# Two of eight norms transposed half on TensorE and half by DMA, a third normalized on GpSimd, in a fused adaLN transformer block

## The chip, the core and the metric

The kernel runs on one core of one Trainium2 chip. Its time is the device time of one execution in microseconds; a lower time is better. The core's engines work side by side, each through its own list of instructions in order, and wait for each other by semaphores: TensorE (PE, matrix products, with weight loads listed as PEld), VectorE (DVE), ScalarE (ACT), GpSimd (POOL) and SyncE (SP), which here only issues DMAs.

## What is computed

The reference is a transformer block over 2048 positions of 512 features: a modulated layer norm, an attention over 8 earlier positions spaced by 2, a gated residual, a second modulated layer norm, a gated GELU feed-forward network with 1792 inner features, and a second gated residual.

```python
mod = (_silu(c) @ w_mod).reshape(c.shape[0], 6, 1, -1)
sa, ca, ga, sb, cb, gb = (mod[:, 0].copy(), ..., mod[:, 5].copy())
h = _layernorm(x, axis=-1) * (1 + ca) + sa
x = x + ga * _A_ref(h, A_wqkv, A_wo)
h = _layernorm(x, axis=-1) * (1 + cb) + sb
x = x + gb * _B_ref(h, B_w_gate, B_w_up, B_w_down)
...
# in _A_ref: 32 heads of 16, window W = 8, dilation 2
idx = pos[:, None] - off[None, :]
mask = idx >= 0
logits = jnp.einsum('bhsd,bhswd->bhsw', q, kg) * scale
logits = jnp.where(mask[None, None, :, :], logits, -1000000000.0)
attn = _softmax(logits, axis=-1)
o = jnp.einsum('bhsw,bhswd->bhsd', attn, vg)
```

## The kernel before

The 2048 positions are worked in four blocks (`sg` 0 to 3) of 512; a block has four chunks of 128 positions, one per `c4`. Each block goes through these steps, and the steps of different blocks overlap:

- **Layer norm 1** (`LN1.sg`): mean and variance of each chunk, by DVE (L430, L431) or by ACT with two accumulating passes (L408, L419); the table `ACT_CH` says which chunks ACT takes. POOL raises the variance to the power of -1/2 (L471, "the root"). DVE subtracts and scales each chunk into `xn` (L448). Then `xn` is transposed so that features lie on partitions, and each of the four groups of 128 features is scaled and shifted by the modulation into `hT`.
- **Transposes.** There are three ways. Block 0's first norm is transposed on PE in two halves (`transp0`, L509) and evicted from PSUM with the scaling by ACT (L545) and DVE (L543). A norm named in `BY_PE` (LN1.1 and LN2.0) is transposed by sixteen PE instructions (L484), and ACT evicts and scales it in four instructions (L527). Every other norm is transposed by one DMA that SP issues (L490); then ACT (L527) or, for LN1.2, POOL (L525) scales `hT` in place.
- **qkv** (L580, L598): groups of four matmuls each, evicted by ACT into `qT`, `kT` and `vT`. `vT` goes to DRAM and comes back in four shifted copies as `V` (L630, L639).
- **Logits**: DVE multiplies q by the shifted k (L659, "the products", `pq`), four times per block; PE sums over the head's features into PSUM (L673). For block 0, DVE adds a mask of large negative numbers to the first 16 positions (L685). Maximum, difference, exponential, sum and division follow on DVE and ACT (L690 to L717).
- **Values**: DVE multiplies the weights by V (L766, "the value products"), PE sums (L780), ACT copies (L791), PE applies `wo` (L801), DVE adds x (L810).
- **Layer norm 2** (`LN2.sg`), in the same way as norm 1, into `h2T`.
- **Feed-forward**: PE's gate and up groups (L834), ACT's GELU and copy (L868, L875), DVE's product (L886), PE's down projection (L846, L858), DVE's residual (L893), SP's store.

At the start PE runs matmuls on a constant tile, the warm-ups (L217), between the first real ones; 32 small matmuls (L348) make the modulation of norm 1.

The order is written out. Every step is a small operation in a generator, and the list `ORDER` names, one number per operation, whose generator goes next. All engines' instructions are emitted in that one order, so each engine's own list is the part of `ORDER` that belongs to it. `take` and `give` count the buffers of a pool; `after` names what must be done. SP's list matters as a queue: it issues loads, stores and DMA transposes one behind the other, and one that waits holds up all behind it. The weights' loads are `Wg` and `Wu` (1792 KB each) and `Wd`.

Of the kernel before, what the change touches and what calls it, by code (L numbers as in the profile page):

```python
# [9 lines left out]
ALU = mybir.AluOpType  # L10
# [96 lines left out]
def kernel(  # L107
# [49 lines left out]
    maskT = const.tile([H, W, 16], F32, name="maskT")  # L157
# [63 lines left out]
    def loads():  # L221
# [28 lines left out]
        def mb(n):  # L250
            return n / 0.333
# [74 lines left out]
    def mods():  # L326
# [15 lines left out]
        for b in (1, 0):  # L342
# [8 lines left out]
            yield Op("PE", 0.43, f, after=[f"wm{b}", "scT", "w15"], take=[SL["mm"]] if b else [],  # L351
# [86 lines left out]

    def norm_x(key, src, ev, parts=((0, 4),)):
        aa, ab = ACT_CH.get(ev, (0, 0))  # L440
        dv = [c4 for c4 in range(CPS) if not aa <= c4 < ab]
        for c4 in range(CPS):
            def f(c4=c4):
                k = norm_tiles(ev)
                if c4 == 0:
                    B[key] = T("xn", [P, CPS, D], BF16, "xn")
                m, o = (k["mv"][:, c4, 0:1], ALU.subtract) if c4 in dv else (k["s"][:, 1, c4:c4 + 1], ALU.add)
                nc.vector.tensor_scalar(out=B[key][:, c4, :], in0=src()[:, c4, :], scalar1=m,  # L448
                                        scalar2=k["rstd"][:, c4:c4 + 1], op0=o, op1=ALU.mult)
            yield Op("DVE", 0.325, f, after=[f"{ev}.rs{max(a for a, b in parts if a <= c4)}"],  # L450
# [24 lines left out]
    def transp(key, dkey, dtag, ev):  # L475
        if ev in BY_PE:
            for dtp in range(2):
                def f(dtp=dtp):
                    hp = T("att", [P, CPS, 2, P], BF16, "hTp")
                    B[key, dtp] = hp  # L480
                    for c4 in range(CPS):
                        for dd in range(2):
# [3 lines left out]
                         fire=f"{ev}.t{dtp}")  # L486
        else:
# [8 lines left out]
    BY_PE = ('LN1.1', 'LN2.0')  # L496
# [17 lines left out]
    def transp_ev(key, dkey, dtag, sc, bi, ev, dep):  # L514
        pe = ev in BY_PE
        for dtp in range(2):
            for dd in range(2):
                dt = 2 * dtp + dd

                def f(dt=dt, dtp=dtp, dd=dd):  # L520
# [5 lines left out]
                    else:  # L526
# [4 lines left out]
                         give=[SL["att"]] if pe and dd == 1 else [], fire=f"{ev}.h{dt}")  # L531

# [19 lines left out]
    def ln1(sg):  # L552
        ev = f"LN1.{sg}"
        yield from norm(lambda: B["x", sg], lambda c4: [f"x0.{c4 // 2 * 2}"] if sg == 0 else [f"x{sg}"], ev,
                        PARTS0 if sg == 0 else ((0, 4),))
# [3 lines left out]
    def ln1_x(sg):  # L559
        yield from norm_x(("xn1", sg), lambda: B["x", sg], f"LN1.{sg}", PARTS0 if sg == 0 else ((0, 4),))  # L560
# [407 lines left out]
```

## Time and profile before

| what | us |
|---|---|
| median of three runs | 237.67 |
| the three runs | 237.32, 237.67, 238.6 |
| the profiled execution | 237.21 |
| its span, first to last instruction | 235.0 |
| TensorE's granted clock | 1.0 of full speed |

The profile's page gives each engine's busy time and the chain of work that ended last. On a timeline row come the start, the time of the group from its first start to its last end, the engine, the line, the operation, the tiles (written<-read), the shapes and the count; in brackets the engine's idle time before it and what ended it. All times in rows are microseconds from the span's start. A row of the chain has start, time, engine, tile and line.

### The profile page before, as it was taken

To read this page: it belongs to the slowest core of one execution; us is meant where nothing else is said; L and a number is where in the kernel's file an instruction comes from. 1 tells how busy PE (TensorE), PEld (TensorE's weight loads), DVE (VectorE), ACT (ScalarE), POOL (GpSimd) and SP (SyncE) were. 2 spreads that over 40 slices of the span, in tenths; PEclk is the share of its full clock that TensorE was granted. 3 is DMA by queue.
4 is the path that set the end of the run, shared out by engine and by line. 5 is a ranking of instruction groups with operands and counts; after the bars stand their busy time and mean duration, and the time that the engine had idled before them with its cause. 6 is when DMAs were issued, how large, how long until landed. Compare 5 with 4: busy or idle time off the path is not lost.

```text
span 235.0 us, 3679 instructions
## 1 busy us (share of the span) xinstructions
PE 230.8 (98%) x1387; PEld 108.4 (46%) x1387; DVE 170.1 (72%) x238; ACT 150.9 (64%) x286; POOL 17.9 (8%) x43
## 2 busy tenths in 40 slices
PE   7999999999999999999999999999999999999995
PEld 2656454444644444444444444444444444444443
DVE  3899999999969999999899899279296211322222
ACT  4899997887996659937647862447636733367400
POOL 2612351000100000100000010000001000000000
PEclk9999999999999999999999999999999999999999
DMA  6998999999975859753100895320002210000011
GB/s 213 374 267 277 214 207 177 246 307 360 199 184 157 295 149 208 121 113 100 59 0 4 157 196 99 120 62 0 0 3 40 50 45 22 25 0 0 0 47 45
DMA packets 36265, 30.21 MB, mean 129 GB/s; under 512 B 14872, under 2 KB 34328, under 8 KB 36248
## 3 DMA queue, kind: packets, MB, share of 16 engines
q1 hardware_dynamic: 35968, 29.72, 50.7%
q8 instruction: 11, 0.18, 0.3%
q10 hardware_dynamic: 280, 0.26, 0.3%
q14 instruction: 6, 0.05, 0.1%
HBM read 22.37 MB, written 4.98 MB: 116 GB/s over the span
## 4 chain that ended last, share of the span: by engine, by line
PE 96%; ACT 2%; DVE 0%; issue 0%
PE u_ps L834 21%; PE g_ps L834 21%; PE y_ps L846 19%; PE qkv_ps L598 16%; PE x_ps L801 6%; PE LTp L673 3%; PE o_ps L780 3%; PE warm_ps L217 3%; PE y_ps L858 1%; PE hTp L484 1%; PE qkv_ps L580 1%; ACT hT L545 1%; ACT gl L419 1%; ACT LTp L701 0%; PE modT_ps L305 0%; PE modT_ps L348 0%
## 5 line engine op out<-in xcount | busy, mean ns | idle before, releaser
L834 PE MATMUL g_ps<-h,Wg 128*128 128x512 bf16 x224 | 57.5, 379 | 0.0
L834 PE MATMUL u_ps<-h,Wu 128*128 128x512 bf16 x224 | 57.5, 379 | 0.0
L868 ACT ACTIVATE gl<-g_ps 128x512 bf16<-128x512 f32 x56 | 33.5, 599 | 25.4 <-PE g_ps L834 22.1
L875 ACT CAST ub<-u_ps 128x512 bf16<-128x512 f32 x56 | 32.8, 586 | 21.4 <-PE u_ps L834 21.3
L846 PE MATMUL y_ps<-Wd,hht 128*128 128x512 bf16 x210 | 46.3, 379 | 0.0
L598 PE MATMUL qkv_ps<-hT,wqkv 128*128 128x512 bf16 x184 | 41.8, 380 | 0.1
L886 DVE TENSOR_TENSOR hht<-gl,ub 128x512 bf16<-128x512 bf16 x56 | 22.6, 420 | 25.2 <-ACT ub L875 23.2
L659 DVE TENSOR_TENSOR pq<-qT,kT 128x4096 bf16<-128x4096 bf16 x16 | 36.2, 2284 | 0.3 <-PE o_ps L780 0.2
L766 DVE TENSOR_TENSOR pv<-PT,V 128x4096 bf16<-128x4096 bf16 x16 | 35.9, 2283 | 0.0
L834 PEld LDWEIGHTS <-Wu 128*128 128x128 bf16 x224 | 21.6, 98 | 27.2 <-issue 1.9
L834 PEld LDWEIGHTS <-Wg 128*128 128x128 bf16 x224 | 21.6, 98 | 27.1 <-issue 1.7
L846 PEld LDWEIGHTS <-hht 128*128 128x128 bf16 x210 | 20.6, 98 | 24.8
L598 PEld LDWEIGHTS <-wqkv 128*128 128x128 bf16 x184 | 20.3, 114 | 19.6 <-issue 2.3
L893 DVE TENSOR_TENSOR ot<-y_ps,x 128x512 bf16<-128x512 f32 x15 | 10.3, 688 | 22.9 <-PE y_ps L846 22.9
L471 POOL TENSOR_TENSOR rstd<-rstd,neghalf 128x4 f32<-128x4 f32 (+1 forms) x9 | 8.9, 990 | 151.0 <-DVE rstd L460 81.3
L801 PE MATMUL x_ps<-woP,oT 128*128 128x512 bf16 x64 | 15.1, 379 | 0.0
L430 DVE BATCH_NORM_STATS2 st<-x 128x6 f32<-128x512 bf16 x18 | 12.3, 685 | 3.2 <-DMA x<-in_A_x_dram 2.9
L810 DVE TENSOR_TENSOR x<-x_ps,x 128x512 bf16<-128x512 f32 x16 | 10.8, 678 | 3.6 <-PE x_ps L801 3.4
L527 ACT ACTIVATE h<-h,modT,scl 128x512 bf16<-128x512 bf16 x12 | 8.8, 803 | 6.8 <-DMA h<-xn 6.8
L791 ACT CAST oT<-o_ps 128x512 bf16<-128x512 f32 x16 | 9.1, 590 | 3.5 <-PE o_ps L780 3.5
L620 ACT CAST kT<-qkv_ps 128x512 bf16<-128x512 f32 x16 | 9.6, 599 | 1.5 <-PE qkv_ps L598 1.4
L801 PEld LDWEIGHTS <-oT 128*128 128x128 bf16 x64 | 6.9, 109 | 7.1 <-issue 0.4
(84 smaller groups left out, 184.8 us busy)
## 6 DMA issues: line engine op xcount, KB each, us to landing
V<-vscr SPq DMA_DIRECT2D x12, 520.0 KB, 9.4
wm<-in_w_mod_dram SPq DMA_DIRECT2D x6, 512.0 KB, 5.9
vscr<-vT SPq DMA_DIRECT2D x4, 512.0 KB, 4.5
out_dram<-ot SPq DMA_DIRECT2D x15, 128.0 KB, 1.7
Wg<-in_B_w_gate_dram SPq DMA_DIRECT2D x1, 1792.0 KB
Wu<-in_B_w_up_dram SPq DMA_DIRECT2D x1, 1792.0 KB, 18.4
wqkv<-in_A_wqkv_dram SPq DMA_DIRECT2D x3, 512.0 KB, 8.5
x<-in_A_x_dram SPq DMA_DIRECT2D x3, 512.0 KB, 7.6
```

The source lines that it names most:

```text
L430: nc.vector.bn_stats(out=st[:], in_=src()[:, c4, :])
L598: nc.tensor.matmul(ps[:], lhsT=wqkv[blk][:, dt, j::4], rhs=B["hT", sg][:, :, dt, :], start=(dt == 0), stop=(dt == DT - 1))
L659: nc.vector.tensor_tensor(out=pq[:], in0=_ap(B["qT", sg][:, j, :], [[0, W], [1, SG]]), in1=_ap(kT[:, j, sg * SG + 2:sg * SG + 2 + SG], [[2 ...
L766: nc.vector.tensor_tensor(out=t[:], in0=_ap(B["PT", sg][:, 0, :], [[SG, 2], [0, 4], [1, SG]]), in1=_ap(v[:, 0, j, :], [[8, 2], [4 * (SG + ...
L801: nc.tensor.matmul(ps[:], lhsT=B["oT", sg][:, j, c4::CPS] if sg else B["oT", sg][:, j, c4 * P:(c4 + 1) * P], rhs=woP[:, j, :], start=(j == ...
L810: nc.vector.tensor_tensor(out=x[:, c4, :], in0=B["x1ps", sg, c4][:], in1=x[:, c4, :], op=ALU.add)
L834: nc.tensor.matmul(ps[:], lhsT=Wt[:, dt, ft * P:(ft + 1) * P], rhs=B["h2T", sg][:, :, dt, :], start=(dt == 0), stop=(dt == DT - 1))
L846: nc.tensor.matmul(ps[:], lhsT=B["hh", sg, ft][:, c4 * P:(c4 + 1) * P], rhs=B["Wd", ft // 4][:, ft % 4, :], start=(ft == 0), stop=(ft == F ...
L868: nc.scalar.activation(out=gl[:], in_=B["g", sg, ft][:], func=ACT.Gelu_apprx_tanh)
L875: nc.scalar.copy(out=ub[:], in_=B["u", sg, ft][:])
L886: nc.vector.tensor_tensor(out=hh[:], in0=B["gl", sg, ft][:], in1=B["ub", sg, ft][:], op=ALU.mult)
L893: nc.vector.tensor_tensor(out=ot[:], in0=B["y", sg, c4][:], in1=B["x", sg][:, c4, :], op=ALU.add)
```

## The change

- **Half and half.** LN1.1 and LN2.0 leave `BY_PE` and enter `HALF`. Chunks 0 and 1 of `xn` are transposed by a DMA on SP, into half of `hT` (or `h2T`), and scaled there in place by four POOL instructions of 128x256 (`half_ev`). Chunks 2 and 3 are transposed by eight PE instructions into one PSUM tile, and ACT evicts and scales them in four instructions of 128x256. Their norm runs in two parts, each with its own root on POOL. The first matmuls of the block wait for both halves; ACT's evictions wait for both transposes.
- **LN1.3's normalization** (four instructions) moves from DVE to POOL (`X_POOL`).
- **The mask** is a bf16 tile on 128 partitions and is added in PSUM by two small matmuls with an identity, inside the sum of block 0's first logits; the DVE addition goes.
- **The head.** The second half of block 0's x is loaded by SP's queue, second in it, and no longer by ACT's. The warm-ups are 17 in place of 20: ten, three and three ahead of the last modulation matmuls and one behind block 0's transposes, where it was eleven, five and one ahead, two between the halves of the transposes and one behind.
- **The order** of everything is a new list. On POOL, the root of LN1.2 stands between the first and the second scaling of LN1.1. On SP, LN1.1's transpose stands between two weight loads ahead of x of block 3; LN2.0's stands behind the first V load of block 1 and `Wu`, where `Wu` came before that block's V loads. The modulation matmuls of norm 2, the two gate computations and the value sums move a little; the number of the other instructions is the same.

```diff
-    maskT = const.tile([H, W, 16], F32, name="maskT")
+    maskT = const.tile([P, W, 16], BF16, name="maskT")
...
-            yield Op("ACT", 0.46, ldx(0, 2, 4, nc.scalar), fire="x0.2", lat=mb(0.25), dma=True)
...
             yield Op("SP", 0.47, ldx(0, 0, 2), fire="x0.0", lat=mb(0.25))
+            yield Op("SP", 0.47, ldx(0, 2, 4), fire="x0.2", lat=mb(0.25))
...
+    X_POOL = ("LN1.3",)
...
-                nc.vector.tensor_scalar(out=B[key][:, c4, :], in0=src()[:, c4, :], scalar1=m,
-                                        scalar2=k["rstd"][:, c4:c4 + 1], op0=o, op1=ALU.mult)
+                (nc.gpsimd if ev in X_POOL else nc.vector).tensor_scalar(
+                    out=B[key][:, c4, :], in0=src()[:, c4, :], scalar1=m, scalar2=k["rstd"][:, c4:c4 + 1], op0=o, op1=ALU.mult)
...
+        elif ev in HALF:
+            def f():
+                B[dkey] = T(dtag, [P, CPS, DT, P], BF16, dtag)
+                nc.sync.dma_start_transpose(out=B[dkey][:, 0:2].rearrange("p c d s -> p (c d) s"),
+                                            in_=B[key][:, 0:2].rearrange("p c d -> p (c d)"))
+            yield Op("SP", 1.65, f, after=[f"{ev}.x1"], take=[SL[dtag]], fire=f"{ev}.t", lat=0.5)
+
+            def f():
+                B[key, 0] = T("att", [P, DT, 2, P], BF16, "hTp")
+                for dt in range(DT):
+                    for c4 in range(2):
+                        nc.tensor.transpose(B[key, 0][:, dt, c4, :], B[key][:, 2 + c4, dt * P:(dt + 1) * P], ident[:])
+            yield Op("PE", 0.445, f, after=[f"{ev}.x3", "ident"], take=[SL["att"]], give=[SL["xn"]], fire=f"{ev}.t1")
...
-    BY_PE = ('LN1.1', 'LN2.0')
+    BY_PE = ()
+
+    HALF = ('LN1.1', 'LN2.0')
+
+    HALF_POOL = ('LN1.1', 'LN2.0')
...
+        if ev in HALF:
+            for dt in range(DT):
+                def f(dt=dt):
+                    nc.scalar.activation(out=B[dkey][:, 2:4, dt, :], in_=B[key, 0][:, dt, :, :], func=ACT.Identity,
+                                         scale=sc(dt), bias=bi(dt))
+                yield Op("ACT", 0.455, f, after=[f"{ev}.t1", f"{ev}.t"] + dep, give=[SL["att"]] if dt == DT - 1 else [],
+                         fire=f"{ev}.h{dt}")
+            return
...
+    def half_ev(dkey, sc, bi, ev, dep):
+        for dt in range(DT):
+            def f(dt=dt):
+                o = B[dkey][:, 0:2, dt, :]
+                if ev in HALF_POOL:
+                    nc.gpsimd.tensor_scalar(out=o, in0=o, scalar1=sc(dt), scalar2=bi(dt), op0=ALU.mult, op1=ALU.add)
+                else:
+                    nc.scalar.activation(out=o, in_=o, func=ACT.Identity, scale=sc(dt), bias=bi(dt))
+            yield Op("POOL" if ev in HALF_POOL else "ACT", 0.44 if ev in HALF_POOL else 0.47, f, after=[f"{ev}.t"] + dep,
+                     fire=f"{ev}.hp{dt}")
...
+                        if sg == 0 and j == 0:
+                            nc.tensor.matmul(B["LT", 0][0:H, 4 * t:4 * t + 4, 0:16], lhsT=ident[:, 0:H],
+                                             rhs=maskT[:, 4 * t:4 * t + 4, :], start=False, stop=False, tile_position=(0, 0))
...
-        if sg == 0:
-            def f():
-                L = B["LT", 0][0:H, :, 0:16]
-                nc.vector.tensor_tensor(out=L, in0=L, in1=maskT[:], op=ALU.add)
-            yield Op("DVE", 0.32, f, after=["lp.0", "consts"], fire="lm.0")
...
-    pl.spawn(warmup(13, 20))
+    pl.spawn(warmup(13, 17))
```

More of the change, by code (lines that the diff above doesn't have):

```diff
@@ L350, in f @@
                                          start=(kt == 0), stop=(kt == 3))
-            yield Op("PE", 0.43, f, after=[f"wm{b}", "scT", "w15"], take=[SL["mm"]] if b else [],
+            yield Op("PE", 0.43, f, after=[f"wm{b}", "scT", "w11"], take=[SL["mm"]] if b else [],
                      give=[] if b else [SL["prod"]], fire=f"mp{b}")
@@ L447, in f @@
                 m, o = (k["mv"][:, c4, 0:1], ALU.subtract) if c4 in dv else (k["s"][:, 1, c4:c4 + 1], ALU.add)
-                nc.vector.tensor_scalar(out=B[key][:, c4, :], in0=src()[:, c4, :], scalar1=m,
-                                        scalar2=k["rstd"][:, c4:c4 + 1], op0=o, op1=ALU.mult)
-            yield Op("DVE", 0.325, f, after=[f"{ev}.rs{max(a for a, b in parts if a <= c4)}"],
+                (nc.gpsimd if ev in X_POOL else nc.vector).tensor_scalar(
+                    out=B[key][:, c4, :], in0=src()[:, c4, :], scalar1=m, scalar2=k["rstd"][:, c4:c4 + 1], op0=o, op1=ALU.mult)
+            yield Op(*(("POOL", 0.77) if ev in X_POOL else ("DVE", 0.325)), f, after=[f"{ev}.rs{max(a for a, b in parts if a <= c4)}"],
                      take=[SL["xn"]] if c4 == 0 else [], fire=f"{ev}.x{c4}")
@@ L554, in ln1 @@
         yield from norm(lambda: B["x", sg], lambda c4: [f"x0.{c4 // 2 * 2}"] if sg == 0 else [f"x{sg}"], ev,
-                        PARTS0 if sg == 0 else ((0, 4),))
+                        PARTS0 if sg == 0 or f"LN1.{sg}" in HALF else ((0, 4),))
     PARTS0 = ((0, 2), (2, 4))
     def ln1_x(sg):
-        yield from norm_x(("xn1", sg), lambda: B["x", sg], f"LN1.{sg}", PARTS0 if sg == 0 else ((0, 4),))
+        yield from norm_x(("xn1", sg), lambda: B["x", sg], f"LN1.{sg}", PARTS0 if sg == 0 or f"LN1.{sg}" in HALF else ((0, 4),))
     def ln1_ev(sg):
@@ L564, in ln1_ev, with ln1_evh @@
                              f"LN1.{sg}", ["mod01"])
+    def ln1_evh(sg):
+        yield from half_ev(("hT", sg), lambda d: mod01[:, 4 + d:5 + d], lambda d: mod01[:, d:d + 1], f"LN1.{sg}", ["mod01"])
     def ln1_ev0(onv):
@@ L601, in qkv @@
             tk = {0: [SL["q"]], 1: [], 2: [SL["vs"]]}[blk] if j == 0 else []
-            yield Op("PE", 0.865, f, after=[f"LN1.{sg}.h{d}" for d in (("0.1", "1.0", "3.1") if sg == 0 else (2, 3))] + [f"wqkv{blk}"], take=[SL["mm"]] + tk,
+            yield Op("PE", 0.865, f, after=[f"LN1.{sg}.h{d}" for d in (("0.1", "1.0", "3.1") if sg == 0 else (2, 3))] + ([f"LN1.{sg}.hp3"] if f"LN1.{sg}" in HALF else []) + [f"wqkv{blk}"], take=[SL["mm"]] + tk,
                      give=[SL["hT"]] if last else [], fire=f"qp.{sg}.{blk}.{j}")
@@ L814, in ln2 @@
         ev = f"LN2.{sg}"
-        yield from norm(lambda: B["x", sg], lambda c4: [f"x1.{sg}.{c4}"], ev)
+        yield from norm(lambda: B["x", sg], lambda c4: [f"x1.{sg}.{c4}"], ev, PARTS0 if ev in HALF else ((0, 4),))
     def ln2_x(sg):
-        yield from norm_x(("xn2", sg), lambda: B["x", sg], f"LN2.{sg}")
+        yield from norm_x(("xn2", sg), lambda: B["x", sg], f"LN2.{sg}", PARTS0 if f"LN2.{sg}" in HALF else ((0, 4),))
     def ln2_ev(sg):
@@ L822, in ln2_ev, with ln2_evh @@
                              lambda d: modT[:, d:d + 1], f"LN2.{sg}", ["mod3", "mod4"])
+    def ln2_evh(sg):
+        yield from half_ev(("h2T", sg), lambda d: scl[:, d:d + 1], lambda d: modT[:, d:d + 1], f"LN2.{sg}", ["mod3", "mod4"])
     LAST = ((0, 384), (384, 512))
     def ffn_mm(sg):
-        h2 = [f"LN2.{sg}.h3"]
+        h2 = [f"LN2.{sg}.h3"] + ([f"LN2.{sg}.hp3"] if f"LN2.{sg}" in HALF else [])
         for ft in range(FT):
@@ L930 @@
         for n, g in (("sa1", lambda q: norm_act(lambda: B["x", q], lambda c4: [f"x{q}"] if q else ["x0.2", "x0.0"], f"LN1.{q}")),
-                     ("sa2", lambda q: norm_act(lambda: B["x", q], lambda c4: [f"x1.{q}.{c4}"], f"LN2.{q}")), ("ln1", ln1), ("ln1x", ln1_x), ("t1", lambda q: transp(("xn1", q), ("hT", q), "hT", f"LN1.{q}") if q else transp0(("xn1", 0), "LN1.0")), ("h1", lambda q: ln1_ev(q) if q else ln1_ev0(False)), ("qkv", qkv),
+                     ("sa2", lambda q: norm_act(lambda: B["x", q], lambda c4: [f"x1.{q}.{c4}"], f"LN2.{q}")), ("ln1", ln1), ("ln1x", ln1_x), ("t1", lambda q: transp(("xn1", q), ("hT", q), "hT", f"LN1.{q}") if q else transp0(("xn1", 0), "LN1.0")), ("h1", lambda q: ln1_ev(q) if q else ln1_ev0(False)), ("h1h", lambda q: ln1_evh(q) if f"LN1.{q}" in HALF else iter(())), ("h2h", lambda q: ln2_evh(q) if f"LN2.{q}" in HALF else iter(())), ("ln2a", lambda q: rst(f"LN2.{q}", 0, 2, []) if f"LN2.{q}" in HALF else iter(())), ("qkv", qkv),
                      ("qev", qkv_ev), ("v", vload), ("pq", logits), ("lmm", logits_mm), ("soft", soft), ("ptd", lambda q: pt_dma(q) if q in PT_DMA else iter(())), ("pv", pv), ("pvmm", pv_mm), ("pvev", pv_ev), ("x1mm", x1_mm),
```

71 rows, old and new, of the table ORDER are left out of this document.

## The prediction

> **What bounds the kernel now.** I read the page's header and chain of waits first, then the list of what TensorE (PE) waited for.
>
> ```profile
> span 235.0 us, 3679 instructions
> PE 230.8 (98%) x1387; PEld 108.4 (46%) x1387; DVE 170.1 (72%) x238; ACT 150.9 (64%) x286; POOL 17.9 (8%) x43
> ```
>
> ```profile
> engine line waited for: us in total, times, longest us
> PE warm_ps L217 <- DVE gB L212: 1.2, 1, 1.2
> PE qkv_ps L580 <- ACT hT L545: 0.2, 1, 0.2
> ```
>
> PE is busy for 98% and after the first 11 us waits for nobody. So every microsecond of PE work removed is gained, and every new wait in front of PE is paid in full. The profiled execution took 237.21 us: the span and 2.2 us around it. The median of the runs, 237.67, is 0.46 above it. The windows of ten microseconds say where a second engine is full too:
>
> ```profile
> 20.00:30.00 10.00, 10.00 (x111) 5.48 (x110) 10.00 (x9) 9.94 (x26) 2.52 (x1) 1.00 0.89 215
> 40.00:50.00 10.00, 10.00 (x90) 4.94 (x90) 10.00 (x5) 7.94 (x14) 0.00 (x0) 1.00 0.96 214
> ```
>
> After the window's length come PE, weight loads, DVE, ACT and POOL, then the clock, the DMA share and GB/s. From 20 to 30 us DVE is as full as PE: whatever delays DVE there reaches PE.
>
> **Head: 17 warm-ups, x on one queue.**
>
> ```profile
> 1.24 4.88 PE L217 MATMUL warm_ps<-gB 128*128 128x512 bf16 x11 [1.24 <-DVE gB L212]
> 9.23 1.48 ACT L545 ACTIVATE hT<-hTp,mod 128x256 bf16<-128x256 bf16 x3 [0.92 <-PE hTp L509]
> 9.44 0.73 DVE L543 TENSOR_SCALAR hT<-hTp,mod 128x256 bf16<-128x256 bf16 x2 [0.30 <-PE hTp L509]
> 10.31 1.05 DVE L543 TENSOR_SCALAR hT<-hTp,mod 128x256 bf16<-128x256 bf16 x3 [0.15 <-PE hTp L509]
> 10.76 1.80 PE L580 MATMUL qkv_ps<-hT,wqkv 128*128 128x256 bf16 x15 [0.16 <-ACT hT L545]
> 12.39 0.81 PE L598 MATMUL qkv_ps<-hT,wqkv 128*128 128x512 bf16 x3
> ```
>
> A cold warm-up costs 4.88/11 = 0.44. The new order has 16 instead of 17 ahead of the last modulation matmuls, so the ACT evictions can start at 9.23 - 0.44 = 8.8 and end at 10.3. Four pairs of 256-wide matmuls remain behind the third of them; at (12.39 - 10.76)/15 = 0.109 each that is 0.87, and L598 could start at 11.2 instead of 12.39. DVE no longer has two warm-ups between its two groups: 9.0 + 0.73 + 1.05 = 10.8, against 11.36. I take -0.9 for PE, with -0.4 (the one cold warm-up, if the modulation weights land later behind one more load in SP's queue) and -1.2 as ends; DVE is 0.55 ahead.
>
> **Transposes taken from PE.** LN1.1 and LN2.0 keep half of their sixteen transposes on PE:
>
> ```profile
> 20.50 0.89 PE hTp L484 x16
> 62.48 0.47 PE hTp L484 x8
> 63.81 0.45 PE hTp L484 x8
> 28.34 0.98 PE LTp L673 x16
> ```
>
> Half of 0.89 is -0.45, and half of 0.47 + 0.45 is -0.46. The mask costs PE two matmuls of 64 columns; a 512-column one of the same tile costs 0.98/16 = 0.06, so both are between 0 and 0.12, taken as +0.1. What DVE loses with it (0.28) comes below. Widening the mask's memsets falls into POOL's idle time before its first reciprocal root. These PE terms sum to -0.9 - 0.91 + 0.1 = -1.7.
>
> **LN1.1's other half: SP, then POOL, then DVE.** The new chain is: two normalized chunks, a DMA transpose of half size, four POOL scalings of 256 elements (`hp0` to `hp3`), then the first qkv group of block 1. On POOL the root of LN1.2 stands between `hp0` and `hp1`, and DVE's four normalizations of LN1.2 wait for that root; behind them stand the products `pq`, which PE's logits need.
>
> ```profile
> 18.20 1.05 DVE L448 TENSOR_SCALAR xn<-x,mv,rstd 128x512 bf16<-128x512 bf16 x3
> 18.37 1.25 POOL L471 TENSOR_TENSOR rstd<-rstd,neghalf 128x4 f32<-128x4 f32 x1 [3.15 <-DVE rstd L465]
> 20.95 8.89 DVE L659 TENSOR_TENSOR pq<-qT,kT 128x4096 bf16<-128x4096 bf16 x4
> 27.48 3.00 POOL L525 TENSOR_SCALAR hT<-hT,mod 128x512 bf16<-128x512 bf16 x1 [7.87 <-PE qkv_ps L598]
> L525 POOL TENSOR_SCALAR hT<-hT,mod x4: 768/769/3002, 27.5 to 32.0; 128x512 bf16<-128x512 bf16 x4
> hT<-xn SPq DMA_TRANSPOSE x2, 4.4
> ```
>
> Before, this root (1.25) ran beside LN1.1's normalizations. Now the LN1.1 ones come earlier in DVE's queue and nothing independent is left: DVE stands idle for one root, +1.2. Second, the scalings. The first L525 scaling, started at 27.48 under the last of four products, took 3.00 instead of 0.77 and ended about one scaling after the product's end at 29.84: one engine kept the other out. Half-size scalings cost half of 0.77, say 0.4. `hp1` to `hp3` are ready at the very moment at which DVE's normalizations are; one of the two must wait, so DVE's products start between 0 and 2.2 (what that one scaling lost) later. I take the three scalings end to end, +1.2.
>
> The Trainium skill (SBUF — State Buffer, "Who interferes with whom") says that a DVE instruction with two SBUF inputs, or a `tensor_scalar` in a two-port mode, and a GpSimd instruction reading SBUF shut each other out for a whole instruction, whoever is first. The 3.00 us row agrees for the products; no row isolates the normalizations. By the page this term is the full 1.2; if normalizations don't collide it is 0.
>
> The third product of the four ended at 20.95 + 3 x 8.89/4 = 27.6. Now it ends at 27.6 - 0.55 + 1.2 + 1.2 = 29.5. PE needed it at 28.34 + 0.49 = 28.8 and now arrives at 28.8 - 0.9 - 0.45 + 0.1 = 27.6. **Stall: 1.9** (0.7 without exclusion). This contains any wait of PE at the first qkv group, a little earlier. All that holds if the half transpose lands in time for `hp0`: a full one takes 4.4, a half one between 2.2 and 4.4, taken as 3.2; at 4.4 it delays the root, and DVE, by another 0.8.
>
> **The third norm on POOL and the mask, in between.**
>
> ```profile
> 29.76 0.28 DVE L685 TENSOR_TENSOR LTp<-LTp,maskT 32x128 f32<-32x128 f32 x1
> 37.14 1.28 DVE L448 TENSOR_SCALAR xn<-x,sums,rstd 128x512 bf16<-128x512 bf16 x4
> 38.50 2.87 SPq L490 DMA_TRANSPOSE hT<-xn  x1
> 48.15 2.71 PE qkv_ps L598 x12
> ```
>
> DVE is relieved of 0.28 + 1.28 = 1.56, which eats most of its 1.85 delay before the value products. LN1.3's normalizations take 4 x 0.77 = 3.1 on POOL, so its transpose is issued about 1 us later than 38.50, or 3 if a product gets in between. Block 3's matmuls start in the L598 group at 48.15, after one group of block 2, at 49.0; transpose (4.4) and ACT's four scalings (2.8 below) after 39.5 end at 46.7. The cover is 2.3 us. I cost it at nothing; were it gone, at most 1.
>
> **LN2.0's other half.**
>
> ```profile
> 44.85 0.97 SPq L223 DMA_DIRECT2D Wu<-in_B_w_up_dram  x1
> Wu<-in_B_w_up_dram SPq DMA_DIRECT2D x1, 1792.0 KB, 18.4
> 50.63 4.01 SPq L639 DMA_DIRECT2D V<-vscr  x3
> V<-vscr SPq DMA_DIRECT2D x1, 520.0 KB, 6.3
> 58.00:60.00 2.00, 2.00 (x12) 1.02 (x9) 1.90 (x6) 2.00 (x5) 0.18 (x1) 1.00 1.10 206
> 60.87 0.73 DVE L448 TENSOR_SCALAR xn<-x,sums,rstd 128x512 bf16<-128x512 bf16 x2
> 63.04 2.79 ACT L527 ACTIVATE h<-hTp,modT,scl 128x512 bf16<-128x512 bf16 x4
> 65.99 0.86 PE g_ps L834 x4
> ```
>
> SP's queue changes here: Wu's load now stands behind the first V load of block 1, which waits for the block's V buffer (issued at 50.63), and directly ahead of the half transpose. Wu landed at 44.85 + 18.4 = 63.25 with the DMA engines full. With one V load ahead (520 KB at 206 GB/s: 2.5) it lands near 65.8, and the transpose, if it goes through the same queue behind it, near 66.5. If it overtakes, it is issued right after the first two normalizations, which end at 61.6 today and up to one root (1.2) earlier if their root is taken ahead of the other pair's, and lands 3.2 later, at 63.6 to 64.8. Behind the landing come POOL's four scalings (1.6) and, in parallel, ACT's four half evictions, which wait for the same landing (2.79 for full ones; about 1.9 for half). So the first g matmul can start between 65.5 and 68.5; PE arrives at 65.99 - 1.25 + 1.9 - 0.46 = 66.2. Stall between 0 and 2.3; I take **1.8**, as Wu's row, the nearest, shows a queue full until then. ACT's qkv evictions stand behind those waiting scalings; they are late with them.
>
> The Trainium skill (DMA: Bandwidth & Descriptors, "Queues, rings and completion order") has SP own one ring on each DMA engine, consumed in order. No row of before shows a transpose behind so large a load. By that rule the stall is 2.3; without it 0.
>
> **Sum.** 237.21 - 0.9 - 0.91 + 0.1 + 1.9 + 1.8 = 239.2; on the runs' median, 0.4 more, about **239.5 us**.
>
> **Rivals.**
> *Forecast: both stalls appear.* 239.5, own range 238.4 to 242.3 (upwards: late first transpose +0.8, full queue +0.5, exclusion 2.2 instead of 1.2, half of the head's gain; downwards: head -0.3, second stall 0.8 shorter). Chance 0.50.
> *The covers hold.* DVE's root and POOL's scalings find gaps and the half transpose lands early: 237.67 - 1.7 + 0.2 = 236.2, faster. For it: PE's waits show how well everything fits today. Against: DVE at 10.00 of 10.00 has no gap to give. It decides where the POOL chain fits inside the 1.2 us between PE's old and new arrival. Chance 0.15.
> *One stall only.* First alone: 237.67 - 1.7 + 1.9 = 237.9; second alone with the unavoidable 0.7: 238.5. No measurable change. Chance 0.27.
> *POOL is starved.*
>
> ```profile
> 23.90 4.44 PE qkv_ps L598 x20
> ```
>
> DVE's normalizations win, the products follow without a gap, and `hp1` to `hp3` come only after the third: 27.6 - 0.55 + 1.2 + 1.2 = 29.5, while PE started block 1 at 23.9 and wants it at 23.9 - 1.25, and 0.5 less for the logits that now stand behind, about 22. Stall 7.5: about 237.67 - 1.7 + 7.5 + 1.8 = 245. The 3.00 row speaks for it; that POOL needs no semaphore after its root and DVE does speaks against. Chance 0.08.
>
> **How the numbers follow.** Measuring tells about 0.5%, 1.2 us, from no change. Faster: the covers hold, 0.15. Same: one stall, 0.27. Slower: forecast and starvation, 0.58. The range runs from 236.2, the middle of the faster case, to 243.0, above the forecast's own end, leaving out starvation and half of the faster case. Where the cases slower than today are most of the chance, the likeliest's own range is 238.4 to 242.3.
>
> **What would show it.** PE should have a wait near 27 us ended by `pq`, and one ahead of the first g matmul ended by ACT's or POOL's scalings of LN2.0; DVE an idle stretch of about 1.2 near 20 us ended by POOL's root; POOL's 256-wide scalings about 0.4, some stretched; L598 starting at 11.2 to 12.0. Wrong I would be if PE waits nowhere for more than 0.3 after 12 us (then it is faster by 1.5), or if one wait of several microseconds at block 1's first qkv group appears.

## The result, and the profile after

The changed kernel took 241.1 us (median of four runs, 240.13 to 242.0), beside 237.89 for the kernel before (four runs): a ratio of 1.0137 with a 95% interval of 1.0094 to 1.0181. So it is slower by 3.2 us, on the side that was forecast and 1.6 us beyond the forecast of 239.5. Its profiled execution took 240.13, of which the span is 238.4; it is the fastest of the four. Below, medians are over all runs, while ratios leave out runs over 1.5% longer than the kernel's fastest, which had a lower granted clock; where the two say different things, the ratio holds.

The head of the page and TensorE's (PE's) list of waits, for the changed kernel:

```profile
span 238.4 us, 3659 instructions
PE 230.6 (97%) x1370; PEld 106.9 (45%) x1370; DVE 170.2 (71%) x234; ACT 150.6 (63%) x286; POOL 27.4 (11%) x57
```

```profile
engine line waited for: us in total, times, longest us
PE g_ps L876 <- DVE ot L935: 1.5, 1, 1.5
PE LTp L715 <- DVE pq L701: 1.4, 2, 0.8
PE warm_ps L218 <- DVE gB L213: 1.2, 1, 1.2
PE modT_ps L349 <- DMA wm<-in_w_mod_dram: 0.5, 2, 0.3
PE modT_ps L306 <- DMA wm<-in_w_mod_dram: 0.5, 1, 0.5
```

By the page PE has 17 matmul instructions fewer and yet is busy as long. Beside the 1.2 us at the start, which both kernels have, four new lines stand there: two on the modulation weights, one on VectorE's (DVE's) products, one on its outputs. Where the time went is read from the start of the same matmuls in both timelines of PE:

| the first matmul of | before | after | difference |
|---|---|---|---|
| block 0's 512-wide q, k, v (L598, now L640) | 12.39 | 12.35 | -0.04 |
| the long q, k, v run behind block 0's last logits | 29.25 | 31.48 | +2.23 |
| block 0's gate, g.0.0 | 65.82 | 67.42 | +1.60 |
| block 0's y | 98.19 | 99.86 | +1.67 |
| block 1's y | 141.80 | 145.31 | +3.51 |
| the end of the span | 235.0 | 238.4 | +3.4 |

Each column is one execution. Two steps cost time: the first 31 us and the stretch between block 0's y and block 1's. The head first. Rows of PE, ScalarE (ACT) and DVE's timelines in the changed kernel (start, time, engine, line, what; in brackets the idle time before and what ended it):

```profile
7.49 0.55 PE L349 MATMUL modT_ps<-scT,wm 128*128 128x1 bf16 x16 [0.29 <-DMA wm<-in_w_mod_dram]
8.97 0.55 PE L349 MATMUL modT_ps<-scT,wm 128*128 128x1 bf16 x16 [0.26 <-DMA wm<-in_w_mod_dram]
10.03 1.69 DVE L582 TENSOR_SCALAR hT<-hTp,mod 128x256 bf16<-128x256 bf16 x5 [0.30 <-PE hTp L529]
12.35 8.19 PE L640 MATMUL qkv_ps<-hT,wqkv 128*128 128x512 bf16 x36
```

PE asks earlier for the modulation weights and they are not there; DVE's evictions end at 11.72, where before they ended at 11.36. Nothing of the warm-up that was saved reaches L640 in this execution. Then the first stall:

```profile
16.18 1.32 SPq L493 DMA_TRANSPOSE hT<-xn  x1
...
20.57 0.56 POOL L566 TENSOR_SCALAR hT<-hT,mod 128x256 bf16<-128x256 bf16 x1 [4.99 <-DMA hT<-xn]
21.10 1.01 POOL L474 TENSOR_TENSOR rstd<-rstd,neghalf 128x4 f32<-128x4 f32 x1
22.10 1.70 POOL L566 TENSOR_SCALAR hT<-hT,mod 128x256 bf16<-128x256 bf16 x3
...
22.14 1.23 DVE L451 TENSOR_SCALAR xn<-x,mv,rstd 128x512 bf16<-128x512 bf16 x2 [2.06 <-POOL rstd L474]
23.30 0.97 DVE L451 TENSOR_SCALAR xn<-x,sums,rstd 128x512 bf16<-128x512 bf16 x2
24.18 8.89 DVE L701 TENSOR_TENSOR pq<-qT,kT 128x4096 bf16<-128x4096 bf16 x4
...
26.52 0.61 PE L715 MATMUL LTp<-pq,Mph 128*32 128x512 bf16 x8 [0.83 <-DVE pq L701]
30.93 0.62 PE L715 MATMUL LTp<-pq,Mph 128*32 128x512 bf16 x8 [0.53 <-DVE pq L701]
```

Read it as a chain. SP issues the half transpose at 16.18; GpSimd (POOL) gets it at 20.57, 4.4 us later. POOL scales `hp0` first and only then takes LN1.2's root, so DVE stands idle for 2.06. Then DVE's four normalizations run against `hp1` to `hp3` and take 1.23 + 0.97 = 2.20, where before two pairs took 0.74 + 0.73:

```profile
19.65 0.74 DVE L448 TENSOR_SCALAR xn<-x,mv,rstd 128x512 bf16<-128x512 bf16 x2
20.30 0.73 DVE L448 TENSOR_SCALAR xn<-x,sums,rstd 128x512 bf16<-128x512 bf16 x2
```

The products `pq` start at 24.18 instead of 20.95, and PE waits for them twice. Ahead of 31.48 PE also waits 0.48 for the third modulation load.

The second stall, ahead of g.0.0, is nearly absent:

```profile
62.30 1.28 SPq L493 DMA_TRANSPOSE h<-xn  x1
...
66.05 2.18 POOL L566 TENSOR_SCALAR h<-h,scl,modT 128x256 bf16<-128x256 bf16 x4 [1.98 <-ACT qT L660]
...
67.42 1.24 PE L876 MATMUL g_ps<-h,Wg 128*128 128x512 bf16 x4
```

The last scaling ends at 66.05 + 2.18 = 68.2. Four such matmuls in a row take 1.02 (the row at 116.39 below); the four of g.0.0 are spread over 1.24, so the wait inside them is 0.22. The third stall stands in no part of the prediction:

```profile
107.85 4.48 DVE L701 TENSOR_TENSOR pq<-qT,kT 128x4096 bf16<-128x4096 bf16 x2
112.25 1.28 DVE L935 TENSOR_TENSOR ot<-y_ps,x 128x512 bf16<-128x512 f32 x2
113.45 2.28 DVE L701 TENSOR_TENSOR pq<-qT,kT 128x4096 bf16<-128x4096 bf16 x1
115.65 0.68 DVE L935 TENSOR_TENSOR ot<-y_ps,x 128x512 bf16<-128x512 f32 x1
...
116.39 1.02 PE L876 MATMUL g_ps<-h,Wg 128*128 128x512 bf16 x4 [1.46 <-DVE ot L935]
```

The kernel before, at the same place:

```profile
101.70 0.68 DVE L893 TENSOR_TENSOR ot<-y_ps,x 128x512 bf16<-128x512 f32 x1
...
106.26 0.68 DVE L893 TENSOR_TENSOR ot<-y_ps,x 128x512 bf16<-128x512 f32 x1
106.85 2.28 DVE L659 TENSOR_TENSOR pq<-qT,kT 128x4096 bf16<-128x4096 bf16 x1
109.05 0.68 DVE L893 TENSOR_TENSOR ot<-y_ps,x 128x512 bf16<-128x512 f32 x1
```

`ot` reads block 0's y out of PSUM and so frees the buffers that block 1's gate and up matmuls write. Before, DVE writes two outputs ahead of block 3's first product and then alternates; the new `ORDER` puts two products ahead of the first output, and PE stands for 1.46. No other part of the change touches this place: only the written-out order does.

### The profile page after: what moved, and what is told of

The parts are those of the page before. It is cut to its first block, busy times and chain, and to the rows that moved or that the text cites. A ratio compares the mean times of both kernels' runs of the same rounds, so it can differ in the third digit from the quotient of the medians.

```text
span 238.4 us, 3659 instructions
## 1 busy us (share of the span) xinstructions
PE 230.6 (97%) x1370; PEld 106.9 (45%) x1370; DVE 170.2 (71%) x234; ACT 150.6 (63%) x286; POOL 27.4 (11%) x57
## 3 DMA queue, kind: packets, MB, share of 16 engines
HBM read 22.37 MB, written 4.98 MB: 115 GB/s over the span
## 4 chain that ended last, share of the span: by engine, by line
PE 60%; DVE 20%; issue 6%; ACT 6%; DMA 5%; POOL 2%; SPq 1%; DVEq 0%; ACTq 0%
PE u_ps L876 17%; PE g_ps L876 17%; PE y_ps L888 14%; DVE pq L701 7%; PE qkv_ps L640 5%; DVE pv L805 3%; PE x_ps L840 3%; DMA wm<-in_w_mod_dram 3%; DVE xn L451 2%; DMA hT<-xn 2%; PE o_ps L819 2%; DVE st L431 2%; PE y_ps L900 1%; ACT ub L917 1%; ACT gl L420 1%
## 5 line engine op out<-in xcount | busy, mean ns | idle before, releaser
L640 PE MATMUL qkv_ps<-hT,wqkv 128*128 128x512 bf16 x184 | 41.8, 380 | 0.0
L640 PEld LDWEIGHTS <-wqkv 128*128 128x128 bf16 x184 | 20.1, 114 | 19.7 <-issue 2.6
L474 POOL TENSOR_TENSOR rstd<-rstd,neghalf 128x2 f32<-128x2 f32 (+1 forms) x11 | 9.6, 870 | 144.8 <-DVE rstd L463 89.5
L431 DVE BATCH_NORM_STATS2 st<-x 128x6 f32<-128x512 bf16 x18 | 12.4, 687 | 2.7 <-DMA x<-in_A_x_dram 2.5
L660 ACT CAST qT<-qkv_ps 128x512 bf16<-128x512 f32 x16 | 9.2, 585 | 2.6 <-PE qkv_ps L640 2.6
L409 ACT ACTIVATE gl<-x 128x512 bf16<-128x512 bf16 x14 | 8.8, 633 | 3.1 <-DMA x<-in_A_x_dram 2.2
```

Source lines behind the costliest of these rows:

```text
L431: nc.vector.bn_stats(out=st[:], in_=src()[:, c4, :])
L640: nc.tensor.matmul(ps[:], lhsT=wqkv[blk][:, dt, j::4], rhs=B["hT", sg][:, :, dt, :], start=(dt == 0), stop=(dt == DT - 1))
```

## The experiments

All are built from the changed kernel, but for e8, which is built from the kernel before. Each was run in five rounds beside the kernel before, whose medians were 237.7 to 237.9. A ratio and its interval are against the kernel before. The diffs of the order name the operations, not the numbers of the list.

**e1: x0.2 on ACT's queue again.**

```
 ACT's queue:
+    x0.2
     c
 SP's queue:
     x0.0
-    x0.2
     wm1, wm0
```

> The changed kernel with one thing undone: the second half of block 0's x is loaded by ACT's queue again, ahead of c. If the one queue made the modulation weights late (they ended TensorE's two waits of 0.29 and 0.26 us near 7 and 9 us), both waits go, the first 512-wide qkv matmuls start at 11.4 to 12.0 instead of 12.35, DVE's block 0 evictions end near 11.0 instead of 11.7, and the time falls by 0.5 to 0.9 us. If the weights are late for another reason (three warm-ups and their places), the two waits stay and the time is the same within 0.3 us.

Measured: 239.67, ratio 1.0071 (1.0048 to 1.0095), about 1.4 less than the changed kernel and more than expected. L640 starts at 11.69. Of the two waits for the modulation weights one went, and the other grew; the third load's wait grew too:

```profile
8.32 0.55 PE L349 MATMUL modT_ps<-scT,wm 128*128 128x1 bf16 x16 [0.66 <-DMA wm<-in_w_mod_dram]
23.45 0.55 PE L306 MATMUL modT_ps<-scT,wm 128*128 128x1 bf16 x16 [1.24 <-DMA wm<-in_w_mod_dram]
```

The queue is part of the head's loss and not all of it: the weights land near 8.3 even so, about when the kernel before asks for them, and PE now asks 0.66 sooner.

One execution's head proves little here. In the profiled executions of the builds from the changed kernel, the seven with x0.2 on SP's queue start L640 at 11.53 to 12.73: the changed kernel, e4, e5, e7 and e11 at 12.27 or later, e2 and e3 at 11.62 and 11.53, although the program of their head is the same. The five with it on ACT's queue (e1, e6, e9, e10, e12) start L640 at 11.42 to 11.85. So the early start is regular with ACT's queue and occasional with SP's. Where in the kernel the 1.4 is gained is not shown: e1's profiled execution is the slowest of its six, with a span 0.1 shorter than the changed kernel's.

**e2: LN1.2's root ahead of `hp0`.**

```
 POOL's order:
-    LN1.1.hp0, LN1.2.rs0
+    LN1.2.rs0, LN1.1.hp0
     LN1.1.hp1, LN1.1.hp2, LN1.1.hp3
```

> The changed kernel with one instruction moved on POOL: the root of LN1.2 stands ahead of the first scaling of LN1.1 instead of behind it. If DVE's idle 2.06 us near 20 us is the wait for the root behind the late half transpose, it shrinks to about 1.1, the products start at about 23.2 instead of 24.2, TensorE's waits for pq fall from 1.36 to 0.5 or less, and the time falls by 0.7 to 1.0 us. If the scalings that shut out DVE's normalizations are what counts, the products start within 0.3 us of 24.2 and the time is the same.

Measured: 240.15, ratio 1.0095 (1.0073 to 1.0118), about 1.0 less. DVE's timeline:

```profile
20.47 1.23 DVE L451 TENSOR_SCALAR xn<-x,mv,rstd 128x512 bf16<-128x512 bf16 x2 [1.12 <-POOL rstd L474]
21.62 1.21 DVE L451 TENSOR_SCALAR xn<-x,sums,rstd 128x512 bf16<-128x512 bf16 x2
```

The idle time falls from 2.06 to 1.12, which is one root; the normalizations stay slow at 2.4 for the four. One of the causes of the first stall is the place of the root, as expected. PE's waits for `pq`, however, fall only from 1.4 to 1.1 and not to 0.5. And of the products' earlier start (22.75 instead of 24.18), 0.7 is this execution's earlier head.

**e3: block 0's outputs ahead of block 3's products on DVE.**

```
 DVE's order:
-    s1.2, ri.2, p.2, pq.3.0, pq.3.1, ot.0.0, ot.0.1, pq.3.2, ot.0.2, pq.3.3, hh.1.0, ..., ot.0.3
+    ot.0.0, s1.2, ri.2, p.2, ot.0.1, pq.3.0, ot.0.2, pq.3.1, ot.0.3, pq.3.2, pq.3.3
```

> The changed kernel with DVE's residual sums of block 0's output taken ahead of block 3's products (and two stores with them), as in the kernel before. If TensorE's wait of 1.46 us at 115 us is made by that order, it goes and the time falls by 1.3 to 1.7 us. If DVE is simply late there because of what it lost earlier, a wait of over 0.8 us remains at that place or on a product a little later.

Measured: 240.75, ratio 1.012 (1.0091 to 1.015): not told apart from the changed kernel. The wait for `ot` is gone and another, on a product, has its place, the sign that was named for a DVE late from what it lost earlier:

```profile
113.50 0.62 PE L715 MATMUL LTp<-pq,Mph 128*32 128x512 bf16 x8 [1.51 <-DVE pq L701]
```

In PE's order block 3's first two logits stand ahead of g.1.0, and now their products are late. Whether DVE is late or the order is only half mended, e5 decides by changing it on both engines.

**e4: LN1.1 transposed wholly on PE.**

```
-    BY_PE = ()
+    BY_PE = ('LN1.1',)
-    HALF = ('LN1.1', 'LN2.0')
+    HALF = ('LN2.0',)
```

> The changed kernel with LN1.1 transposed wholly on TensorE again (sixteen transposes, four ACT evictions of 512, no POOL scalings, one root), all else as changed. If the half transpose and POOL's scalings make the stall near 20 to 31 us, DVE's idle there falls to 1.2 or less, TensorE's two waits for pq go to under 0.4 together, and the time falls by 1.4 to 2.0 us although TensorE gets 0.45 us of work back. If only the new order makes it, the waits stay and the time rises by 0.2 to 0.5.

Measured: 239.78, ratio 1.0103 (1.007 to 1.0137), about 1.3 less by the medians and 0.8 by the ratios, whose intervals overlap, though PE has eight transposes more. Its waits for `pq` fall from 1.4 to 0.4, with the head as late as in the changed kernel (L640 at 12.34). DVE still stands 1.12 for the root; its four normalizations are back at 0.73 + 0.73. So the half transpose with its scalings is a net loss in this order.

**e5: as e3, and block 3's first logits behind g.1.4 on PE.**

```
 PE's order:
-    y.0.3.1, lp.3.0, lp.3.1, g.1.0, u.1.0, ..., u.1.3, g.1.4
+    y.0.3.1, g.1.0, u.1.0, ..., u.1.3, g.1.4, lp.3.0, lp.3.1
```

> The changed kernel with two moves: block 0's four outputs ot.0.* ahead of block 3's products on VectorE (as in e3), and the two first logits of block 3 on TensorE moved behind the gate matmul g.1.4, where the kernel before has them. Theory (the third stall is one of order on VectorE and TensorE together: six operations, two outputs and two products among them, are asked for in the 4 us ahead of g.1.0, and whichever of them comes last is waited for): with both moved, TensorE waits for neither at 110 to 116 us; the 1.46 us ahead of g.1.0 are gone and no wait of over 0.3 us takes their place there; time 1.4 to 1.7 less than the changed kernel's 241.1, 239.4 to 239.8 (the head may move it by 0.7 in either direction). Rival (VectorE is short of time on this stretch, whatever the order): the 1.5 us come again later, at the logits behind g.1.4 or at a gate matmul whose buffer hh or ot must free; time within 0.5 of 241.1.

Measured: 239.68, ratio 1.0075 (1.0048 to 1.0102), 1.4 less. Between 110 and 116 us the list shows no wait of PE; a wait of 0.40 for a value product comes at 125.19. So the third stall is one of order on the two engines together, and worth 1.4.

**e6: e1, e4 and e5 together.** The diffs are those three.

> The changed kernel with three parts undone or mended: x0.2 on ScalarE's queue again (e1), LN1.1 transposed wholly on TensorE (e4), outputs and logits of the third stall in the order of e5. What is left of the change: LN2.0 half by DMA, LN1.3 applied on GpSimd, the mask by matmul, 17 warm-ups, and the new order elsewhere. Theory (the loss is the sum of these three places, and they add up): 241.1 - 1.4 (e1) - 1.3 (e4) - 1.45 (third stall) = 236.9, that is 0.6 to 1.3 under the kernel before; range 236.3 to 237.8. Rival A (the places share their waits, so that mending one brings out the next: a weight or a product is late at the end anyway): 238.3 or more, no better than before. Rival B (what is left of the change costs something spread over the rest): no single wait over 0.5 us and yet 238 or more.

Measured: 238.4, ratio 1.0023 (1.0006 to 1.0039). The three single gains (1.4, 1.3, 1.4) give 2.7 together, not 4.2: rival A, at its lower edge. What still stands in PE's list:

```profile
PE LTp L714 <- DVE pq L700: 0.7, 2, 0.5
PE modT_ps L348 <- DMA wm<-in_w_mod_dram: 0.6, 1, 0.6
PE o_ps L818 <- DVE pv L804: 0.4, 1, 0.4
```

**e7: LN2.0 transposed wholly on PE.**

```
-    BY_PE = ()
+    BY_PE = ('LN2.0',)
-    HALF = ('LN1.1', 'LN2.0')
+    HALF = ('LN1.1',)
```

> The changed kernel with LN2.0 transposed wholly on TensorE again (LN1.1 stays half by DMA). Theory (the second half transpose is hidden; its stall in the profile is about 0.2 us, while the saved transposes are 8 on TensorE, about 0.45 us): time 240.9 to 241.6, within 0.5 of the changed kernel, and the chain ahead of g.0.0 shows two more pairs of transposes and no wait for the half transpose. Rival (the half transpose through its queue and the scalings on GpSimd cost about 1.8 us there, as the prediction put it): 239.3 to 239.8, 1.3 us or more less than the changed kernel.

Measured: 241.29, ratio 1.0139 (1.0115 to 1.0162): as the changed kernel. The second half transpose costs nothing that can be measured, and gains nothing. With all of LN2.0 on PE and ACT the four matmuls of g.0.0 are spread over 1.24 too.

**e8: the kernel before, with x0.2 on SP's queue.**

```
 ACT's queue:
-    x0.2
     c
 SP's queue:
     x0.0
+    x0.2
     wm1, wm0
```

> The kernel before with one part of the change alone: the second half of x's block 0 on SP's queue behind the first half, ahead of the modulation weights. Theory (the move delays the modulation weights by 0.5 to 1.2 us, whatever the rest of the order): modT's matmuls wait for the weights' DMA or the first q matmul starts 0.3 to 1.0 us later than the 12.39 us of before; time 0.2 to 1.0 over the kernel before. Rival (the weights are late in the changed kernel because its TensorE asks for them earlier, after 12 and not 16 warm-ups; the queue does nothing): here the time is within 0.3 of the kernel before and no wait for weights appears.

Measured: 238.73, ratio 1.0039 (1.0021 to 1.0057): 0.9 slower from this one load. L598 starts at 12.96 instead of 12.39. PE's timeline:

```profile
8.94 0.55 PE L348 MATMUL modT_ps<-scT,wm 128*128 128x1 bf16 x16 [0.69 <-DMA wm<-in_w_mod_dram]
...
17.97 3.70 PE L598 MATMUL qkv_ps<-hT,wqkv 128*128 128x512 bf16 x16 [0.53 <-DMA wqkv<-in_A_wqkv_dram]
```

Of the loads behind it in SP's queue, the modulation weights and the last third of the q, k, v weights come later by at least 0.5 each, since the kernel before waits for neither at an earlier time. Together with e1: the move delays the weights, and PE's earlier demand alone makes them late too.

**e9: e6, and LN1.2's statistics where the kernel before has them.**

```
 DVE's order:
-    LN1.1.x0, LN1.2.st0, LN1.1.x1, pq.0.0, LN1.1.x2, LN1.1.x3, LN1.2.st1, LN1.2.vd0, LN1.2.va0
+    LN1.2.st0, LN1.2.st1, LN1.2.vd0, pq.0.0, LN1.2.va0, LN1.1.x0, LN1.1.x1, LN1.1.x2, LN1.1.x3
     LN1.2.x0, LN1.2.x1, LN1.2.x2, LN1.2.x3, pq.0.1
 ACT's order:
-    LN1.2.sq2, cast qkv.0.0.3, cast qkv.0.1.2, LN1.2.sq3
+    LN1.2.sq2, LN1.2.sq3, cast qkv.0.0.3, cast qkv.0.1.2
```

> e6 with one more move: LN1.2's statistics ahead of the first product of block 0 on VectorE and ScalarE, and LN1.1's four applications behind that product, which is the order of the kernel before there. Theory (what is left of the first stall in e6, two roots of 1.21 and 1.12 us for which VectorE waits and 2 us by which the products of block 0 start late, is order alone): the products start near 21 us and not at 23.04, VectorE's waits for the two roots are under 0.3 us, TensorE's waits for products (0.74 us in e6, with what each costs beside) are gone, time 0.7 to 1.1 less than e6's 238.4: 237.3 to 237.7, at or just under the kernel before. Rival (TensorE waits for something else right after, a weight or block 1's casts on ScalarE): 238.1 to 238.6.

Measured: 237.87, ratio 1.0008 (0.9994 to 1.0022): no difference from the kernel before. LN1.2's root runs beside LN1.1's normalizations again:

```profile
18.12 1.05 DVE L450 TENSOR_SCALAR xn<-x,mv,rstd 128x512 bf16<-128x512 bf16 x3
18.29 1.24 POOL L473 TENSOR_TENSOR rstd<-rstd,neghalf 128x4 f32<-128x4 f32 x1 [3.44 <-DVE rstd L467]
...
20.87 8.89 DVE L700 TENSOR_TENSOR pq<-qT,kT 128x4096 bf16<-128x4096 bf16 x4
```

The products start at 20.87, before 20.95, and PE waits for none of them. The time came out between theory and rival, and a new wait of 0.74 appears ahead of 18.53, for ACT's cast of `qT`, behind which LN1.2's square stood until then.

**e10: all of the change's work on the engines, with the order mended.** The moves of e1, e2 and e5, and of e9's those of LN1.2; LN1.1 stays half by DMA, with its first two normalizations ahead of the product. Of the change's parts only x0.2's queue is undone.

> The changed kernel with all its work, LN1.1 half by DMA and scaled on GpSimd included; mended are x0.2's queue, the third stall's order, and LN1.2's statistics and root, which go ahead as in e9. The products of block 0 now follow on LN1.2's applications at about 21 us, while GpSimd's four 256-wide scalings come with the half transpose at 20 to 20.5 us. Theory (a run of products keeps GpSimd's scalings out, across the boundary between two products too): the scalings run 2 us and more late, the last of them ends after 25 us, TensorE waits over 1.5 us ahead of block 1's first matmuls, where hT's scalings and not the products are named, and the time is 239.5 or more, over 1 us more than e9 (which has 8 more transposes on TensorE, about 0.45 us). Rival (the late root alone made the stall, and the scalings share the memory with the products at a small cost): no wait of over 0.6 us ahead of block 1, time within 0.5 of e9.

Measured: 238.26, ratio 1.0018 (0.9987 to 1.0049): not told apart from the kernel before, nor from e9. The theory fell: POOL was not starved. POOL's and DVE's timelines:

```profile
20.10 2.27 POOL L566 TENSOR_SCALAR hT<-hT,mod 128x256 bf16<-128x256 bf16 x4
...
20.14 1.23 DVE L451 TENSOR_SCALAR xn<-x,mv,rstd 128x512 bf16<-128x512 bf16 x2 [0.58 <-POOL rstd L474]
21.29 1.22 DVE L451 TENSOR_SCALAR xn<-x,sums,rstd 128x512 bf16<-128x512 bf16 x2
22.43 8.88 DVE L701 TENSOR_TENSOR pq<-qT,kT 128x4096 bf16<-128x4096 bf16 x4
```

The four scalings take 2.27, no more than four of 0.56 each. The four normalizations pay instead, 2.45 where e9's took 0.73 + 0.73, and the products, which would have kept POOL out, stand behind them: they start at 22.43, and the last scaling has ended at 20.10 + 2.27 = 22.37.

**e11: LN1.3's normalizations on DVE.**

```
-    X_POOL = ("LN1.3",)
+    X_POOL = ()
 DVE's order:
+    LN1.3.x0, LN1.3.x1, LN1.3.x2, LN1.3.x3
     pq.1.1, pq.1.2
```

> The changed kernel with the applications of LN1.3 on VectorE again, ahead of the product pq.1.1. Theory (this part is hidden behind TensorE both ways; GpSimd had no other work there and VectorE's 1.3 us find room): no new wait of TensorE of over 0.3 us near 35 to 50 us, time within 0.5 of the changed kernel's 241.1. Rival (the 1.3 us of VectorE that it saved were needed, since softmax and products of blocks 0 and 1 follow there): 241.7 or more, with a wait for a product or pv between 40 and 50 us.

Measured: 241.08, ratio 1.0142 (1.0112 to 1.0172), as the changed kernel. But a wait of 0.88 appears:

```profile
53.88 0.61 PE L819 MATMUL o_ps<-pv,Msum 128*32 128x512 bf16 x8 [0.88 <-DVE pv L805]
```

In the changed kernel there is none at these matmuls. So DVE's 1.3 us can reach PE, somewhat later than the rival said, though the time does not show it: in this execution the wait for the third modulation load (0.48 in the changed kernel) was missing. What the part is worth alone stays open, between nothing and 0.9.

**e12: e10 with the cast of `qT` ahead of LN1.2's last square.**

```
 ACT's order:
-    LN1.2.sq3, cast qkv.0.0.3
+    cast qkv.0.0.3, LN1.2.sq3
```

> e10 with one ScalarE move: the cast of qT's fourth tile ahead of LN1.2's last square instead of behind it. TensorE waited 0.74 us for that cast in e9 and e10 (17.8 to 18.8 us), because LN1.2's statistics were pulled ahead of it. Theory (the wait is the price of the pulled square, 0.72 us with its read-out, and nothing stands behind it): the wait falls under 0.15 us, LN1.2's root comes 0.5 us later, which costs TensorE 0 to 0.4 us at the products, and the time is 0.2 to 0.9 less than e10's 238.26: 237.4 to 238.0, no slower than the kernel before. Rival (the first 20 us are bound by ScalarE's chain from x's second load to the casts, so that what the head gains is waited for somewhere): the 0.7 us come again at the next casts or at the products, time within 0.2 of e10.

Measured: 239.38, ratio 1.0039 (1.0017 to 1.006), no gain over e10, and outside what the theory allowed. PE's wait for the cast falls from 0.74 to 0.16, and this comes in its place:

```profile
28.66 0.62 PE L715 MATMUL LTp<-pq,Mph 128*32 128x512 bf16 x8 [0.39 <-DVE pq L701]
29.20 11.83 PE L640 MATMUL qkv_ps<-hT,wqkv 128*128 128x512 bf16 x52
```

In e10 the same 52 matmuls start at 29.71 and take 11.41; the next group starts at 42.47 there and at 42.38 here. The half microsecond is gone by then. The weight loads of the 52 matmuls pause twice in e12 (0.37 ahead of 32.09, 0.25 ahead of 35.69) and not in e10. That a chain through ACT bounds the first 40 us is consistent with this and not shown.

## Why the prediction was right, and where it was not

The sign and the kind were right: slower, since the new order lets new waits in front of PE. That the sum came within 1.6 us is luck, since large errors of opposite sign met. By the marks of the table, the head came out 0.9 worse than forecast, the stretch of the first stall 0.7 worse, that of the second 2.0 better and that of the third 1.8 worse. (239.2 and 0.4 are 239.6; the forecast says about 239.5.)

- **Head, -0.9: failed, measured -0.04 in the profiled execution.** The step that failed is the allowance for x's second half on SP's queue, -0.4 at worst: the modulation weights bound the head, both because PE asks sooner (e1) and because the load now stands ahead of them (e8, 0.9 by itself). The saved warm-up itself does count: with the load back on ACT's queue L640 starts 0.5 to 1.0 ahead of the 12.39 of before, and in e2 and e3 it does so even with SP's.
- **First stall, 1.9: the mechanism was right, its terms were mis-sized.** The three causes are those named. DVE's idle time for the root was put at 1.2 and measured 2.06, since the half transpose took 4.4 and not 3.2; that was the upper bound, and its 0.8 is about the difference. The exclusion was put at 1.2 and measured 0.7 (2.20 against 1.47). The head, taken as 0.55 earlier on DVE, was 0.36 later. From 12.4 to 31.5 us PE lost 2.27 net, the 0.48 for the third modulation load among it, where the sum had -0.45 + 0.1 + 1.9 = 1.55. e2, e4 and e9 confirm the mechanism by taking its causes away.
- **POOL's scaling, 0.4: measured 0.56.** A 256-wide one is not half of a 512-wide one (0.77).
- **LN1.3 on POOL, nothing: right as far as it goes.** No wait came from it. Near 53 us its gain on DVE may be needed (e11).
- **Second stall, 1.8: mis-sized, measured about 0.2.** Two steps were off. The first is Wu's load. It was issued only at 54.08, but it did not last: the DMA engines moved 291 GB/s from 54.08 to 62.30, 2.4 MB, about what the V load and Wu hold together (the sum took 206 GB/s), and from 62.50 to 63.50 they were busy for a share of 0.17. So Wu was all but through when the half transpose was issued at 62.30, and the transpose landed 3.5 later. The Trainium skill's rule that was weighed there (DMA: Bandwidth & Descriptors, "Queues, rings and completion order"), by which the stall was estimated at 2.3, was not put to the test, as hardly anything stood ahead of the transpose any more. The second step is PE's arrival, 67.42 and not 66.2: POOL's last scaling ended at 68.2, close to the 66.5 + 1.6 = 68.1 of the sum, and PE came late enough to see little of it. e7 shows the half transpose to be neutral; in other executions with it the same place costs PE up to 0.8 (e3, g.0.0 spread from 66.28 to 68.14).
- **Third stall: missed.** It cost 1.46 directly, and the difference grows by 1.84 between the two y marks. The prediction followed the parts of the change and took the rest of the new `ORDER` for equal; comparing what each engine runs ahead of each gate matmul would have shown two products ahead of the first output.
- **The rivals.** "The covers hold" fell with DVE's 2.06 of idle time. "One stall only" was nearer than its chance of 0.27: of the two stalls forecast, only the first came. Its 237.9 was missed because the head gained nothing and the third stall came. "POOL is starved" did not happen: the normalizations and the scalings take turns, here and in e10.

e10 settles the large question: with x0.2 back on its queue and the order mended around LN1.2 and block 0's outputs, all the rest of the change leaves the kernel where it was before, within -0.3 to 1.2 us. The load's queue lost 0.9 in the kernel before (e8) and 1.4 in the changed one (e1); the order lost about 2, which is the remainder and no run's own measure. The other parts together neither gain nor lose measurably; the warm-ups and the mask were not run by themselves. None of the mended versions is faster than the kernel before.

## What to carry to other kernels

When a change comes with a new written-out order, read the order of each engine over the whole kernel, not only around the parts that changed: the single dearest wait here, 1.46 us, was far from all of them. Work saved ahead of a load gains nothing unless the load comes earlier too, so look up when the weights land before counting a saved instruction. Where a stall is mended on one engine, look at once which instruction waits next; here three mends worth 1.3 to 1.4 each gave 2.7 together. And do not read a half microsecond off one execution: the same head started L640 anywhere from 11.53 to 12.73.

## What the runs showed of the hardware

POOL's durations in the changed kernel (shortest, median and longest in ns):

```profile
L553 POOL TENSOR_SCALAR hT<-hT,mod x4: 767/769/4347, 29.3 to 35.1; 128x512 bf16<-128x512 bf16 x4
...
L566 POOL TENSOR_SCALAR hT<-hT,mod x4: 558/573/588, 20.6 to 23.2; 128x256 bf16<-128x256 bf16 x4
```

- A scaling that started under a run of products at 29.30 took 4.35 us, to 33.65, although the run had a boundary between two products at 24.18 + 3 x 8.89/4 = 30.85; alone it takes 0.77, so most of it ran after the run's end at 33.07. e10 repeats it: 3.51 for the scaling at 28.37, over a boundary at 29.09. Against normalizations, POOL's scalings were hardly stretched (0.56 to 0.59) and DVE's were, from 0.37 to 0.61 each. The Trainium skill (SBUF — State Buffer, "Who interferes with whom") has the two engines shut each other out for a whole instruction, whoever is first: the normalizations agree with it; the scaling held over a boundary between two products shows one engine keeping the other out for longer than one instruction.
- Half a DMA transpose lands little sooner than a whole one. From issue to landing the changed kernel's two halves took 4.3 (into `hT`, issued at 16.18) and 3.5 (into `h2T`, at 62.30); the whole ones of the kernel before took 4.3 to 4.7, with a median of 4.4. The halves, shortest, median and longest:

```profile
DMA to landing us min/median/max: 3.5/3.9/4.3
```
